# The second feed-forward layer's seven-product chunks: the 256 last token columns of each half, from plain products to seven products of their own

## The chip, the cores and the metric

The kernel runs on one core of a Trainium2 chip. The metric is device microseconds of one execution; a kernel's time is the median of its runs. A core has five engines that run side by side, each through its own queue in order: PE (TensorE, matrix products), DVE (VectorE), ACT (ScalarE), POOL (GpSimd) and SP (SyncE, which issues the transfers). They wait for each other by semaphores.

## The reference

Three stages follow one another: clustered attention over 2 x 8 heads, a mixture of four experts, and a second feed-forward layer. The change is in the last stage, for 1536 tokens, 512 channels and 2048 hidden units:

```python
def _moe2_ref(x, w_in, w_out):
    h = x @ w_in                      # (1536, 512) @ (512, 2048)
    g = np.maximum(0.01 * h, h)
    return (g @ w_out).astype(np.float32)
```

`w_in` and `w_out` come as 64-bit floats; the kernel narrows them to 32 bits itself.

## The kernel before, in words

Every 32-bit operand of a product is split into a high part that TensorE's fp32r format holds and the rest, and a product is three matmuls (high x high, high x low, low x high).

Both feed-forward layers run in chunks of 256 hidden units (`FCH`): 16 chunks for the experts (c = 0 to 15, `N1` = 16), 8 for the second layer (c = 16 to 23). A chunk has a first part, h = x @ w1 with its activation, and a second, h @ w2, which is added to `acc`. The first part comes in two forms. The chunks in `PLAIN` (0, 1, 16, 17, 18) multiply directly: 3 token groups x 2 halves of the hidden units x 12 matmuls of 512 columns. The others call `emit_seven`. It cuts the problem into 2 x 2 blocks (two halves of the channels, two halves of the tokens) and does a Strassen-like scheme with seven block products instead of eight. A block product (`product`) is 6 matmuls. A half has 768 tokens (`HT`); a PSUM bank takes 512 columns, so each product is done for block A, the first 512 columns of each half, and the remaining 256 columns of each half are block B, the narrow block.

For the experts' chunks B goes through seven products too (`some_b` is (A, B)). For the second layer's five seven-product chunks, c = 19 to 23, `some_b` is (A,) and `plain_b(f)` does B directly: for each half f of the hidden units, 12 matmuls of 512 columns, the two halves' 256 columns side by side. `plain_b(0)` stands after the first product of A, `plain_b(1)` ahead of its last.

The sums of token blocks that the seven products need (t1 to t4) don't change over a layer's chunks. `input_sums` makes them once per layer: 14 instructions on DVE and 4 on ACT, 18 steps, which the lists `quota` deal out over the plain chunks. In the second layer: 0 and 4 in the first and second part of chunk 16, 4 and 4 in chunk 17, 3 and 3 in chunk 18.

Behind a result of the first part stands this chain. `h_act`: in the second layer ACT writes 0.01 h to g (L669) and DVE takes the larger (L670), or DVE does both at once where the value lies in SBUF already (L667); in the experts' chunks it is one DVE instruction (L665). Then `split`: ACT writes the high part `hhi` (L126) and POOL the low part `hlo` (L127). The second part (`emit_y2` for the second layer) takes 12 groups of 128 tokens in order, i = 0 to 11, with 6 matmuls each: hhi by w2hi, hhi by w2lo, hlo by w2hi, for both halves of the hidden units. Group i = 4 holds tokens 512 to 639, the first of block B. Each ends in a DVE add to `acc` (L1005 in chunk 16, a copy, L1007 later). Eight PSUM banks are shared; `y_bank` and `BANKS` fix which result takes which, so the ninth group (i = 8) takes the bank that i = 3 had.

The order on each engine is the order in which the code is written. Between the products `some(1)` deals out the steps that prepare the next chunk's weights: `weights_narrow` is one ACT instruction (L179) and four on DVE (L180, L183, L186, L189), each over 128 x 1024 elements. `u2`, `u3` and the like are the scheme's partial sums, in tile `part`; `plus` (L906) adds a bank to them.

Of the kernel before, what the change touches and what calls it, by code (L numbers as in the profile page):

```python
# [66 lines left out]
def attention_moe_kernel(  # L67
# [13 lines left out]
    nc = tc.nc  # L81
    B, H, S, D = q.shape
# [12 lines left out]
    KC = DM // 128  # L95
# [22 lines left out]
    def small(n=None):  # L118
        if n is None:
            n = turns[1]  # L120
            turns[1] += 1
        pool, tag = smalls[n % len(smalls)]
        return pool.tile([128, 512], F32, tag=tag, name=tag)

    def split(hi, lo, src, lo_engine):
        nc.scalar.activation(out=hi, in_=src, func=AF.Copy)  # L126
        lo_engine.tensor_tensor(out=lo, in0=src, in1=hi.bitcast(F32), op=ALU.subtract)  # L127


    xhi = keep.tile([128, KC, NT], F32R, name="xhi")  # L130
    xlo = keep.tile([128, KC, NT], F32R, name="xlo")
# [23 lines left out]
    hbuf, gbuf, pbuf = [], [], []  # L155
# [3 lines left out]
    N1 = len(chunks)  # L159
# [407 lines left out]
    ps = small()  # L567
# [88 lines left out]
    def g_slot(n):  # L656
        return gbuf[n // 2][:, n % 2, :]
# [5 lines left out]
    def h_act(c, g, src, p):  # L663
        if c < N1:
            nc.vector.scalar_tensor_tensor(out=g, in0=src, scalar=0.0, in1=p, op0=ALU.max, op1=ALU.mult)  # L665
        elif src is g:
            nc.vector.scalar_tensor_tensor(out=g, in0=src, scalar=0.01, in1=src, op0=ALU.mult, op1=ALU.max)  # L667
        else:
            nc.scalar.activation(out=g, in_=src, func=AF.Copy, scale=0.01)  # L669
            nc.vector.tensor_tensor(out=g, in0=src, in1=g, op=ALU.max)  # L670

    def h_whole(c, f, src, t0, g=None):

        ts = slice(t0, t0 + 512)
        g = g_next() if g is None else g
        h_act(c, g, src, pbuf[0][:, 0, ts])
        hi, lo = [x[:, f, ts] for x in hbuf[0]]
        split(hi, lo, g, nc.gpsimd)
# [130 lines left out]
    part = ffn.tile([128, 2, NT // 2], F32, name="part")  # L809
# [3 lines left out]
    def bank(n):  # L813
        return psum_f.tile([128, 512], F32, tag=f"z{n}", name=f"z{n}")
# [8 lines left out]
    HT = NT // 2  # L823
# [4 lines left out]
    def input_sums(whole):  # L828

        sub, add = ALU.subtract, ALU.add  # L830
        steps = []

        def tt(out, in0, in1, op):
            steps.append(lambda: nc.vector.tensor_tensor(out=out, in0=in0, in1=in1, op=op))

        cols = slice(0, 512 if whole else HT)

        def parts(n, src):
            hi, lo = t_hi[n][:, :, cols], t_lo[n][:, :, cols]
            steps.append(lambda: nc.scalar.activation(out=hi, in_=src, func=AF.Copy))  # L840
            tt(lo, src, hi.bitcast(F32), sub)

        b11, b12, b21, b22 = [[x.bitcast(F32)[:, :, cols] for x in b] for b in quarters]
        if whole:
            f, g = pbuf[0][:, 0, 0:1024].rearrange("p (k t) -> p k t", k=2), part[:, :, 0:512]
        else:
            f, g = [
                x.bitcast(F32).rearrange("p a b -> p (a b)")[:, 0:NT].rearrange("p (k t) -> p k t", k=2) for x in raw64
            ]
        tt(f, b12[0], b11[0], sub)  # L850
        tt(f, f, b12[1], add)
        tt(f, f, b11[1], sub)
        tt(g, b22[0], f, sub)
        tt(g, g, b22[1], add)
        parts(0, f)
        tt(f, b21[0], g, sub)
        tt(f, f, b21[1], add)
        parts(1, g)
        parts(3, f)
        tt(g, b22[0], b12[0], sub)  # L860
        tt(g, g, b22[1], add)
        tt(g, g, b12[1], sub)
        parts(2, g)
        return steps

    def product(ps, w, x, sub, first=True):

        for k in range(2):
            for i, j in ((0, 0), (0, 1), (1, 0)):
                nc.tensor.matmul(  # L870
                    ps, lhsT=w[i][:, k, :], rhs=x[j][:, k, sub], start=first and k + i + j == 0,
                    stop=k == 1 and i == 1, skip_group_check=True,
                )
# [10 lines left out]
    def emit_seven(c, steps):  # L884

        w = w1s[0]
        a11, a12, a21, a22 = [
            [x[:, 2 * k:2 * k + 2, 128 * f:128 * f + 128] for x in w] for f in range(2) for k in range(2)
        ]
        s1, s2, s3, s4 = [[x[:, n] for x in (shi, slo)] for n in range(4)]  # L890
        t1, t2, t3, t4 = zip(t_hi, t_lo)
        x11, x21, x22 = quarters[0], quarters[2], quarters[3]
        A, B = slice(0, 512), slice(512, HT)
        z = {(A, n): bank(b) for n, b in zip("aebcd", (2, 3, 4, 5, 6))}
        z.update({(B, n): bank(b)[:, 0:256] for n, b in zip("aeb", (0, 1, 7))})
        z[B, "c"], z[B, "d"] = z[B, "b"], z[B, "a"]
        u2, u3 = [{A: part[:, n, A], B: part[:, n, B]} for n in range(2)]
        gB = [g_slot(2), g_slot(3)]

        def some(n):  # L900
            for _ in range(n):
                if steps:
                    steps.pop(0)()

        def plus(out, ps, other):
            nc.vector.tensor_tensor(out=out, in0=ps, in1=other, op=ALU.add)  # L906

        def done(m, f, u, src):
            if m == A:
                h_whole(c, f, src, HT * u, g_slot(0))  # L910
                return
            to = src if f and u else gB[f][:, 256 * u:256 * u + 256]
            h_act(c, to, src, pbuf[0][:, 0, HT * u + 512:HT * u + HT])
            if u == 1:
                hi, lo = [x[:, f, :].rearrange("p (u t) -> p u t", u=2)[:, :, 512:HT] for x in hbuf[0]]
                split(hi, lo, gB[f].rearrange("p (u t) -> p u t", u=2), nc.gpsimd)

        some_b = (A, B) if c < N1 else (A,)

        def plain_b(f):  # L920

            ps = bank(f)
            xs = [x.rearrange("p k (u t) -> p k u t", u=2) for x in (xhi, xlo)]
            for k in range(KC):
                for i, j in ((0, 0), (0, 1), (1, 0)):
                    nc.tensor.matmul(  # L926
                        ps.rearrange("p (u t) -> p u t", u=2), lhsT=w[i][:, k, 128 * f:128 * f + 128],
                        rhs=xs[j][:, k, :, 512:HT], start=k + i + j == 0, stop=k == KC - 1 and i == 1,
                    )
            h_act(c, gB[f], ps, None)  # L930
            hi, lo = [x[:, f, :].rearrange("p (u t) -> p u t", u=2)[:, :, 512:HT] for x in hbuf[0]]
            split(hi, lo, gB[f].rearrange("p (u t) -> p u t", u=2), nc.gpsimd)

        for m in some_b:
            product(z[m, "a"], a11, x11, m)
            nc.scalar.activation(out=u2[m], in_=z[m, "a"], func=AF.Copy)
        weights_split(1)
        some(1)
        if c >= N1:
            plain_b(0)  # L940
            some(1)
        for m in some_b:
            product(z[m, "b"], s2, t2, m)
            plus(u2[m], z[m, "b"], u2[m])
        some(1)
        for m in some_b:
            product(z[m, "a"], a12, x21, m, False)
            done(m, 0, 0, z[m, "a"])
        some(1)
        for m in some_b:  # L950
            product(z[m, "c"], s3, t3, m)
            plus(u3[m], z[m, "c"], u2[m])
        g = g_slot(1)
        c22 = {A: g, B: gB[1][:, 256:512]}
        for m in some_b:
            product(z[m, "e"], a22, t4, m)
            plus(z[m, "e"], z[m, "e"], u3[m])
            if m == A and c < N1:
                done(m, 1, 0, z[m, "e"])
            product(z[m, "d"], s1, t1, m)  # L960
            plus(c22[m], z[m, "d"], u3[m])
        done(B if c < N1 else A, 1, 0, z[B if c < N1 else A, "e"])
        h_act(c, g, g, pbuf[0][:, 0, HT:HT + 512])
        split(hbuf[0][0][:, 1, HT:HT + 512], hbuf[0][1][:, 1, HT:HT + 512], g, nc.gpsimd)
        if c < N1:
            done(B, 1, 1, c22[B])
        else:
            plain_b(1)
        for m in some_b:
            product(z[m, "d"], s4, x22, m, False)  # L970
            plus(z[m, "d"], z[m, "d"], u2[m])
            done(m, 0, 1, z[m, "d"])
# [46 lines left out]
    for c in range(NCH):  # L1019
# [8 lines left out]
        if c in PLAIN:  # L1028
# [6 lines left out]
            if c == N1:  # L1035
                sums_left = input_sums(True)
                quota = [0, 4, 4, 4, 3, 3]
# [7 lines left out]
            for n, (u, f) in enumerate(blocks):  # L1045
                if c > 0:
                    ps = bank(BANKS[u][f])
# [6 lines left out]
                if c == 0:  # L1054
                    ps = both_ps[f]
# [64 lines left out]
```

## Time and profile before

| | |
|---|---|
| median of 3 runs | 1029.95 us (1029.0 to 1031.38) |
| profiled execution, time | 1032.72 us |
| profiled execution, span of the trace | 1031.0 us |
| busy: PE, DVE, POOL, ACT | 1003.8, 715.0, 605.2, 403.8 us |
| mean granted TensorE clock | 0.993 |

A matmul's shown duration overlaps the next one's; what a matmul takes of the engine is the distance between two starts. The time of a row is from the span's start. In a row of several instructions (x2, x3) the busy time is their sum.

### The profile page before, as it was taken

The numbers are of one execution on the slowest core, as the hardware profiler recorded it, in microseconds if no ns is written. First come the engines' busy times: TensorE is split into PE (matmuls) and PEld (weight loads), VectorE is DVE, ScalarE is ACT, GpSimd is POOL, SyncE is SP. The second block draws the span as 40 slices with busy tenths as digits, with TensorE's granted clock in tenths as the row PEclk, the third lists the DMA queues.
The fourth block names the chain that finished last, engine by engine and source line by source line (L and its number), as shares of the span: only waits on it lengthen the run. The fifth ranks groups of instructions, "written<-read, shape, count | busy, mean of one in ns | idle before, by whom it ended". The sixth has DMA issues, their size and how long they took to land.

```text
span 1031.0 us, 15762 instructions
## 1 busy us (share of the span) xinstructions
PE 1003.8 (97%) x6322; PEld 831.3 (81%) x6322; DVE 715.0 (69%) x1066; ACT 403.8 (39%) x562; POOL 605.2 (59%) x460
## 2 busy tenths in 40 slices
PE   7799999999999999999999999999999999999998
PEld 5578888888778888888888888888877888888886
DVE  7698888887778556554565555565678878686664
ACT  3477777775232222221222212222343533334331
POOL 4267777780467657545666546575585646676661
PEclk9799999999999999999999999999999999999999
DMA  7755666540101121011110112012012221212103
GB/s 171 179 109 129 139 140 140 116 124 22 41 21 42 37 56 42 21 41 41 51 42 21 42 41 70 23 55 89 1 41 82 82 82 42 81 41 75 49 1 123
DMA packets 59538, 70.78 MB, mean 69 GB/s; under 512 B 25060, under 2 KB 42088, under 8 KB 59464
## 3 DMA queue, kind: packets, MB, share of 16 engines
q1 hardware_dynamic: 59464, 69.77, 25.4%
q8 instruction: 49, 0.80, 0.3%
q14 instruction: 25, 0.20, 0.1%
HBM read 46.19 MB, written 3.17 MB: 48 GB/s over the span
## 4 chain that ended last, share of the span: by engine, by line
PE 86%; DVE 9%; SPq 2%; issue 1%; POOL 1%; ACT 1%; DMA 0%; DVEq 0%; ACTq 0%; POOLq 0%
PE z L870 24%; PE z L982 8%; PE z L984 8%; PE z L983 8%; PE z L880 6%; PE z L1000 4%; PE z L1002 4%; PE z L1001 4%; PE big L422 3%; PE z L926 3%; PE big L457 3%; PE big L458 2%; DVE m L426 2%; PE small L483 1%; PE small L484 1%; PE small L485 1%
## 5 line engine op out<-in xcount | busy, mean ns | idle before, releaser
L127 POOL TENSOR_TENSOR hlo<-g,hhi 128x512 fp32r<-128x512 f32 x140 | 196.3, 1417 | 143.3 <-ACT hhi L126 138.7
L989 DVE TENSOR_TENSOR acc<-z,acc 128x512 f32<-128x512 f32 x180 | 123.1, 689 | 98.2 <-PE z L984 98.2
L471 POOL TENSOR_TENSOR plo<-p,phi 128x768 f16<-128x768 f32 x84 | 137.9, 1653 | 80.0 <-ACT phi L470 51.9
L126 ACT ACTIVATE hhi<-g 128x512 fp32r<-128x512 f32 x140 | 86.9, 632 | 197.5 <-DVE g L665 154.5
L982 PE MATMUL z<-hhi,w2hi 128*128 128x512 f32 x384 | 153.0, 398 | 1.1 <-DVE acc L987 1.1
L984 PE MATMUL z<-hlo,w2hi 128*128 128x512 f32 x384 | 151.5, 394 | 1.1 <-POOL hlo L127 1.1
L983 PE MATMUL z<-hhi,w2lo 128*128 128x512 f32 x384 | 150.7, 392 | 0.0
L199 POOL TENSOR_TENSOR w2lo<-w2raw,w2hi 128x512 fp32r<-128x512 f32 x46 | 59.0, 1305 | 132.8 <-ACT w2hi L196 132.8
L426 DVE TENSOR_REDUCE m<-big 128x1 f32<-128x768 f32 x96 | 90.0, 951 | 23.7 <-PE big L422 23.4
L460 ACT ACTIVATE p<-big 128x768 f32<-128x768 f32 x96 | 77.4, 808 | 35.0 <-PE big L458 29.6
L984 PEld LDWEIGHTS z<-hlo,w2hi 128*128 128x128 f32 x384 | 72.1, 188 | 19.9 <-POOL hlo L127 1.5
L982 PEld LDWEIGHTS z<-hhi,w2hi 128*128 128x128 f32 x384 | 72.1, 188 | 17.5 <-DVE acc L987 1.5
L983 PEld LDWEIGHTS z<-hhi,w2lo 128*128 128x128 f32 x384 | 72.1, 188 | 16.5
L1000 PE MATMUL z<-w2hi,hhi 128*128 128x512 f32 x192 | 76.5, 398 | 1.2 <-DVE acc L1005 1.0
L1002 PE MATMUL z<-w2hi,hlo 128*128 128x512 f32 x192 | 76.1, 396 | 0.0
L1001 PE MATMUL z<-w2lo,hhi 128*128 128x512 f32 x192 | 76.0, 396 | 0.0
L199 POOL TENSOR_TENSOR w1lo<-w1raw,w1hi 128x512 fp32r<-128x512 f32 x48 | 74.0, 1564 | 1.7 <-ACT w1hi L196 1.6
L457 PE MATMUL big<-qka 128*128 128x512 f32 x192 | 71.7, 374 | 1.6 <-DVE pair L127 0.8
L906 DVE TENSOR_TENSOR part<-z,part 128x512 f32<-128x512 f32 x66 | 38.1, 578 | 50.6 <-PE z L870 50.0
L196 ACT ACTIVATE shi<-sums 128x1024 fp32r<-128x1024 f32 x19 | 20.1, 1060 | 125.6 <-POOL sums L217 125.6
L1007 DVE TENSOR_TENSOR acc<-z,acc 128x512 f32<-128x512 f32 x84 | 56.6, 684 | 17.4 <-PE z L1002 16.6
L665 DVE SCALAR_TENSOR_TENSOR g<-z,pb 128x512 f32<-128x512 f32 x92 | 52.2, 568 | 22.7 <-PE z L870 12.9
(210 smaller groups left out, 2585.1 us busy)
## 6 DMA issues: line engine op xcount, KB each, us to landing
qkb<-pair SPq DMA_DIRECT2D x32, 384.0 KB
w1raw<-in_moe_w_dram SPq DMA_DIRECT2D x16, 512.0 KB
w2raw<-in_moe_w_dram SPq DMA_DIRECT2D x16, 512.0 KB
w1raw<-in_moe_w_in_dram SPq DMA_DIRECT2D x8, 1024.0 KB
w2raw<-in_moe_w_out_dram SPq DMA_DIRECT2D x8, 1024.0 KB
qka<-pair SPq DMA_DIRECT2D x16, 384.0 KB
vraw<-in_v_dram SPq DMA_DIRECT2D x16, 192.0 KB
pb<-pe_rows SPq DMA_DIRECT2D x4, 768.0 KB
```

The lines of the kernel that those rows point to most:

```text
L127: lo_engine.tensor_tensor(out=lo, in0=src, in1=hi.bitcast(F32), op=ALU.subtract)
L199: nc.gpsimd.tensor_tensor(out=lo[:, x], in0=src[:, x], in1=hi.bitcast(F32)[:, x], op=ALU.subtract)
L426: nc.vector.tensor_reduce(out=m_t[t][:, j:j + 1], in_=ps[:, 0:S], op=ALU.max, axis=AX.X)
L471: (nc.vector if plo_on_vector else nc.gpsimd).tensor_tensor(out=plo, in0=p, in1=phi, op=ALU.subtract)
L870: nc.tensor.matmul(ps, lhsT=w[i][:, k, :], rhs=x[j][:, k, sub], start=first and k + i + j == 0, stop=k == 1 and i == 1, skip_group_check=True,
L982: nc.tensor.matmul(ps, lhsT=whi[:, f, ks], rhs=hi[:, f, us], start=f == 0, stop=False)
L983: nc.tensor.matmul(ps, lhsT=wlo[:, f, ks], rhs=hi[:, f, us], start=False, stop=False)
L984: nc.tensor.matmul(ps, lhsT=whi[:, f, ks], rhs=lo[:, f, us], start=False, stop=f == NF - 1)
L989: nc.vector.tensor_tensor(out=a, in0=ps, in1=a, op=ALU.add)
L1000: nc.tensor.matmul(ps, lhsT=hi[:, f, ts], rhs=whi[:, f, :], start=f == 0, stop=False)
L1001: nc.tensor.matmul(ps, lhsT=hi[:, f, ts], rhs=wlo[:, f, :], start=False, stop=False)
L1002: nc.tensor.matmul(ps, lhsT=lo[:, f, ts], rhs=whi[:, f, :], start=False, stop=f == NF - 1)
```

## The change

In the five chunks c = 19 to 23, block B goes through the seven products as in the experts' chunks; `plain_b` is gone. `input_sums` makes the second layer's sums for all 768 columns of a half instead of the first 512.

```diff
@@ input_sums @@
-        cols = slice(0, 512 if whole else HT)
+        cols = slice(0, HT)
...
-            f, g = pbuf[0][:, 0, 0:1024].rearrange("p (k t) -> p k t", k=2), part[:, :, 0:512]
+            f, g = pbuf[0][:, 0, :].rearrange("p (k t) -> p k t", k=2), part[:, :, :]
@@ emit_seven @@
-        some_b = (A, B) if c < N1 else (A,)
-
-        def plain_b(f):
-
-            ps = bank(f)
-            xs = [x.rearrange("p k (u t) -> p k u t", u=2) for x in (xhi, xlo)]
-            for k in range(KC):
-                for i, j in ((0, 0), (0, 1), (1, 0)):
-                    nc.tensor.matmul(
-                        ps.rearrange("p (u t) -> p u t", u=2), lhsT=w[i][:, k, 128 * f:128 * f + 128],
-                        rhs=xs[j][:, k, :, 512:HT], start=k + i + j == 0, stop=k == KC - 1 and i == 1,
-                    )
-            h_act(c, gB[f], ps, None)
-            hi, lo = [x[:, f, :].rearrange("p (u t) -> p u t", u=2)[:, :, 512:HT] for x in hbuf[0]]
-            split(hi, lo, gB[f].rearrange("p (u t) -> p u t", u=2), nc.gpsimd)
-
-        for m in some_b:
+        for m in (A, B):
             product(z[m, "a"], a11, x11, m)
...
         if c >= N1:
-            plain_b(0)
             some(1)
-        for m in some_b:
+        for m in (A, B):
             product(z[m, "b"], s2, t2, m)
             plus(u2[m], z[m, "b"], u2[m])
...
-        done(B if c < N1 else A, 1, 0, z[B if c < N1 else A, "e"])
+        if c >= N1:
+            done(A, 1, 0, z[A, "e"])
+        done(B, 1, 0, z[B, "e"])
         h_act(c, g, g, pbuf[0][:, 0, HT:HT + 512])
         split(hbuf[0][0][:, 1, HT:HT + 512], hbuf[0][1][:, 1, HT:HT + 512], g, nc.gpsimd)
-        if c < N1:
-            done(B, 1, 1, c22[B])
-        else:
-            plain_b(1)
-        for m in some_b:
+        done(B, 1, 1, c22[B])
+        for m in (A, B):
             product(z[m, "d"], s4, x22, m, False)
             plus(z[m, "d"], z[m, "d"], u2[m])
             done(m, 0, 1, z[m, "d"])
```

DVE's queue in one of these chunks, from the first narrowing step of the next chunk's w1 to the partial sum that the last product of A waits for (the second L906 into `g_3471`). Before:

```order
L180 TENSOR_SCALAR w1raw<-w1raw 128x1024
L906 TENSOR_TENSOR part<-z_8847,part 128x512
L183 TENSOR_SCALAR w1raw<-w1raw 128x1024
L670 TENSOR_TENSOR g_3471<-z_8845,g_3471 128x512
L186 SCALAR_TENSOR_TENSOR w1raw<-w1raw_4249,w1raw 128x1024
L906 TENSOR_TENSOR part<-z_8848,part 128x512
L906 TENSOR_TENSOR z_8846<-z_8846,part 128x512
L906 TENSOR_TENSOR g_3471<-z_8849,part 128x512
```

The same stretch of DVE's queue now; the rows of 128x256 are the narrow block's:

```order
L180 TENSOR_SCALAR w1raw<-w1raw 128x1024
L906 TENSOR_TENSOR part<-z_8872,part 128x512
L906 TENSOR_TENSOR part<-z_8877,part 128x256
L183 TENSOR_SCALAR w1raw<-w1raw 128x1024
L670 TENSOR_TENSOR g_3471<-z_8870,g_3471 128x512
L670 TENSOR_TENSOR g_4247<-z_8875,g_4247 128x256
L186 SCALAR_TENSOR_TENSOR w1raw<-w1raw_4249,w1raw 128x1024
L906 TENSOR_TENSOR part<-z_8873,part 128x512
L906 TENSOR_TENSOR part<-z_8877,part 128x256
L906 TENSOR_TENSOR z_8871<-z_8871,part 128x512
L906 TENSOR_TENSOR g_3471<-z_8874,part 128x512
```

Three instructions of the narrow block came in ahead of that partial sum, one of them an L670 that waits for ACT.

ACT's queue at the end of such a chunk, from the high part of A's partial sum on (L126 rows with 128x2x256 are block B's; `g_4247` is B's buffer). Before:

```order
L126 ACTIVATE hhi_3469<-g_3471 128x512 x2
L669 ACTIVATE g_4247<-z_8929 128x512
L126 ACTIVATE hhi_3469<-g_4247 128x2x256
L669 ACTIVATE g_3471<-z_8849 128x512
L126 ACTIVATE hhi_3469<-g_3471 128x512
L179 ACTIVATE w2raw<-w2raw_4250 128x1024
```

And now:

```order
L126 ACTIVATE hhi_3469<-g_3471 128x512
L669 ACTIVATE g_4247<-z_8876 128x256
L126 ACTIVATE hhi_3469<-g_3471 128x512
L126 ACTIVATE hhi_3469<-g_4247 128x2x256
L669 ACTIVATE g_3471<-z_8874 128x512
L126 ACTIVATE hhi_3469<-g_3471 128x512
L669 ACTIVATE g_4247<-z_8875 128x256
L126 ACTIVATE hhi_3469<-g_4247 128x2x256
L179 ACTIVATE w2raw<-w2raw_4250 128x1024
```

The last high part that the chunk makes was A's (second token half); now it is B's, for the first half of the hidden units and both token halves.

## Rows read from the trace of the kernel before

**Rows 1.** The page: busy time of PE, and the chain that ended last.
```profile
PE 1003.8 (97%) x6322; PEld 831.3 (81%) x6322; DVE 715.0 (69%) x1066; ACT 403.8 (39%) x562; POOL 605.2 (59%) x460
PE 86%; DVE 9%; SPq 2%; issue 1%; POOL 1%; ACT 1%; DMA 0%; DVEq 0%; ACTq 0%; POOLq 0%
```
**Rows 2.** Windows: stretch, length, busy us (instructions) of PE PEld DVE ACT POOL, clock, DMA.
```profile
320.19:334.89 14.70, 14.70 (x85) 12.87 (x84) 10.44 (x17) 3.65 (x6) 8.52 (x6) 1.00 0.20 62
779.37:798.42 19.05, 17.88 (x74) 13.23 (x72) 19.00 (x22) 4.32 (x6) 10.13 (x6) 1.00 0.18 56
815.20:832.00 16.80, 16.80 (x74) 13.50 (x73) 15.88 (x20) 5.39 (x7) 6.62 (x4) 1.00 0.04 17
898.07:913.40 15.33, 15.33 (x68) 12.44 (x67) 9.46 (x13) 7.36 (x11) 7.02 (x6) 1.00 0.08 30
```
**Rows 3.** Timeline of PE, an experts' chunk: start, us, instruction, [idle before <-releaser].
```profile
320.19 0.39 PE L870 MATMUL z<-xhi,w1hi 128*128 128x512 f32 x1
321.59 0.28 PE L870 MATMUL z<-xhi,w1hi 128*128 128x256 f32 x1
322.29 0.40 PE L870 MATMUL z<-thi,shi 128*128 128x512 f32 x1
```
**Rows 4.** Timeline of DVE, second part of chunk 16.
```profile
787.07 1.21 DVE L834 TENSOR_TENSOR pb<-xhi 128x1024 f32<-128x1024 f32 x1
...
790.44 0.68 DVE L1005 COPY acc<-z 128x512 f32<-128x512 f32 x1
791.04 1.69 DVE L834 TENSOR_TENSOR pb<-pb,xlo 128x1024 f32<-128x1024 f32 x1
```
**Rows 5.** Timeline of PE, the same stretch.
```profile
791.26 0.47 PE L1000 MATMUL z<-w2hi,hhi 128*128 128x512 f32 x1 [0.48 <-DVE acc L1005]
```
**Rows 6.** L834 by itself: ns min/median/max, first and last start, form (the experts' sums).
```profile
L834 DVE TENSOR_TENSOR w1raw<-w1raw,xlo x3: 1742/1742/1770, 275.8 to 295.8; 128x1536 f32<-128x1536 f32 x3
```
**Rows 7.** Timeline of ACT, the seven-product part of chunk 20.
```profile
899.67 0.60 ACT L936 ACTIVATE part<-z 128x512 f32<-128x512 f32 x1 [4.89 <-PE z L870]
...
901.11 1.12 ACT L179 ACTIVATE w1raw<-w1raw 128x1024 f32<-128x1024 f32 x1
902.48 0.60 ACT L669 ACTIVATE g<-z 128x512 f32<-128x512 f32 x1 [0.25 <-PE z L926]
903.91 0.63 ACT L126 ACTIVATE hhi<-g 128x512 fp32r<-128x512 f32 x1 [0.83 <-DVE g L670]
```
**Rows 8.** Timeline of DVE, the same stretch.
```profile
903.18 0.69 DVE L670 TENSOR_TENSOR g<-z,g 128x512 f32<-128x512 f32 x1 [4.22 <-ACT g L669]
...
906.98 1.21 DVE L186 SCALAR_TENSOR_TENSOR w1raw<-w1raw,w1raw 128x1024 int32<-128x1024 int32 x1
...
908.89 0.70 DVE L906 TENSOR_TENSOR z<-z,part 128x512 f32<-128x512 f32 x1
909.50 0.68 DVE L906 TENSOR_TENSOR g<-z,part 128x512 f32<-128x512 f32 x1
```
**Rows 9.** Timeline of POOL, the same stretch.
```profile
901.29 2.54 POOL L199 TENSOR_TENSOR w2lo<-w2raw,w2hi 128x512 fp32r<-128x512 f32 x2 [3.89 <-ACT w2hi L196]
904.62 1.29 POOL L127 TENSOR_TENSOR hlo<-g,hhi 128x512 fp32r<-128x512 f32 x1 [0.78 <-ACT hhi L126]
```
**Rows 10.** Groups by line and form, 690 to 1031 us, narrow forms: xcount | busy, mean ns.
```profile
L906 DVE TENSOR_TENSOR part<-z,part 128x256 f32<-128x256 f32 x4 | 1.7, 425 | 0.1
...
L936 ACT ACTIVATE part<-z 128x256 f32<-128x256 f32 x2 | 0.8, 384 | 0.2
```
**Rows 11.** Timeline of POOL in chunks 17 and 21.
```profile
804.74 1.28 POOL L127 TENSOR_TENSOR hlo<-g,hhi 128x512 fp32r<-128x512 f32 x1
...
948.59 2.14 POOL L127 TENSOR_TENSOR hlo<-g,hhi 128x512 fp32r<-128x512 f32 x1 [0.85 <-ACT hhi L126]
```
**Rows 12.** Timeline of DVE in chunks 17 and 21.
```profile
805.01 1.56 DVE L180 TENSOR_SCALAR w1raw<-w1raw 128x1024 f32<-128x1024 f32 x1 [1.72 <-ACT w1raw L179]
...
948.35 1.22 DVE L189 SCALAR_TENSOR_TENSOR w1raw<-w1raw,w1raw 128x1024 int32<-128x1024 int32 x1
```

More of the change, by code (lines that the diff above doesn't have):

```diff
@@ L949, in emit_seven @@
         some(1)
-        for m in some_b:
+        for m in (A, B):
             product(z[m, "c"], s3, t3, m)
@@ L954, in emit_seven @@
         c22 = {A: g, B: gB[1][:, 256:512]}
-        for m in some_b:
+        for m in (A, B):
             product(z[m, "e"], a22, t4, m)
@@ L961, in emit_seven @@
             plus(c22[m], z[m, "d"], u3[m])
-        done(B if c < N1 else A, 1, 0, z[B if c < N1 else A, "e"])
+        if c >= N1:
+            done(A, 1, 0, z[A, "e"])
+        done(B, 1, 0, z[B, "e"])
         h_act(c, g, g, pbuf[0][:, 0, HT:HT + 512])
         split(hbuf[0][0][:, 1, HT:HT + 512], hbuf[0][1][:, 1, HT:HT + 512], g, nc.gpsimd)
-        if c < N1:
-            done(B, 1, 1, c22[B])
-        else:
-            plain_b(1)
-        for m in some_b:
+        done(B, 1, 1, c22[B])
+        for m in (A, B):
             product(z[m, "d"], s4, x22, m, False)
```

## The prediction, made before the changed kernel ran

> **What bounds the kernel now.** I read the page first: PE is busy 97% of the span and 86% of the chain that ended last is PE's [rows 1]. So the kernel is PE from end to end, and a change is worth what it takes from PE's queue less the gaps it opens there. The windows come next, for where PE has gaps and how full DVE is in the stretches the change touches [rows 2]. In the seven-product part of chunk 20 (898.07 to 913.40) PE has no gap: 15.33 of 15.33 us, with DVE at 9.46. An experts' chunk, where the narrow block already takes the seven products, is 14.70 us, without a gap either. One stretch is different: the second part of chunk 16 lasts 19.05 us with DVE busy for 19.00 of it. There DVE is the bound, and PE waits for banks: the ninth group starts at 791.26 after DVE's copy of the fourth, which ended at 790.44 + 0.68 [rows 4, 5]. Last I read the timelines of ACT, DVE and POOL in chunk 20, because the change lengthens their chains [rows 7 to 9].
>
> **PE's own work.** A product on 512 columns takes 321.59 - 320.19 = 1.40 us, one on 256 columns 322.29 - 321.59 = 0.70 us [rows 3]: half the columns, half the time. Removed per chunk: 24 matmuls of 512 columns at 1.40 / 6, 5.60 us. Added: 42 of 256 columns at 0.70 / 6, 4.95 us (seven products). That is -0.65 us a chunk, -3.2 us in five, if PE never waits; it agrees with 15.33 against 14.70.
>
> **The sums of token blocks.** 14 DVE instructions grow from 1024 to 1536 elements. At 1024 one takes 1.21 us, or 1.69 beside POOL [rows 4]; the experts' sums at 1536 take 1.742 [rows 6]. So +0.53 each. Four stand in the second part of chunk 16, in the queue between the copies that free PE's banks; DVE has nothing to hide them under, and PE gets 4 x 0.53 = 2.1 us of further gaps. Longer instructions also meet POOL more often there, at most one more difference of 1.69 - 1.21; I take 2.3, bounds 1.6 (three of the four stand ahead of the copy of i = 4) to 2.6. The other ten stand in chunks 17 and 18. In the second part of chunk 17 DVE is busy 15.88 of 16.80 us without a PE gap [rows 2]; PE's groups run five banks ahead of the copies, some 5 x 1.4 us, and two more times 0.53 fit under that. I cost them at nothing; without that cover it would be 10 x 0.53 = 5.3 us, and up to 0.5 of it I keep for the range.
>
> **The chains in a chunk.** The steps between engines, from chunk 20: ACT starts 0.20 us after a product's end (899.67 against 898.07 + 1.40); DVE 0.10 after ACT (902.48 + 0.60 to 903.18); ACT 0.04 after DVE (903.87 to 903.91); POOL 0.08 after ACT (904.54 to 904.62) [rows 7 to 9]; PE 0.14 after DVE [rows 4, 5]. On DVE an instruction starts 0.09 before the last one's end [rows 8]. The narrow L906 takes 0.43, the narrow copy on ACT 0.38 [rows 10]; I use these for narrow L670 and L669 too. POOL's instructions take 1.27 each [rows 9].
>
> DVE and POOL hold each other up where both work in SBUF. L180 at 805.01 met a POOL instruction that ran from 804.74 to 806.02, and ended 0.55 us after it. At 948.35 L189 came first: POOL's instruction of 948.59 took 2.14 and ended 1.16 us after L189's end [rows 11, 12]. So whoever starts first finishes, the other then takes nearly its whole time.
>
> Now the new order, in us from the block's first matmul. (1) ACT's narrow copy waits for its product until 2.31 and pushes L179 from 3.04 to 3.55, done at 4.67; POOL's two w2lo follow from 3.72. (2) DVE's L180 meets the first w2lo and ends at 5.54, the two L906 end at 6.5, L183 meets the second w2lo (to 6.70) and ends at 7.25, L670 of A ends at 7.85. (3) ACT's queue holds L126 of A before L669 of B, so B's L669 runs 8.44 to 8.82 and DVE, whose next instruction is L670 of B, sits idle for 1 us and ends it at 9.35. (4) Meanwhile POOL has begun A's hlo (8.61 to 9.88); L186, which in the trace came ahead of POOL (906.98), now comes behind it and ends at 11.0. (5) Four more L906 follow, and the sum that the last product of A accumulates onto ends at 13.17. PE is there at 12.56 and starts at 13.31: **a gap of 0.75 us**. Before, that sum ended at 909.50 + 0.68, 12.1 [rows 8], and the 2.8 us of `plain_b(1)` stood in between. Queued behind it are B's last product and the whole second part.
>
> (6) The second part starts at 13.31 + 1.37 + 0.71 = 15.39, and its group i = 4, the first of the narrow block, at 15.39 + 4 x 1.40 = 21.0. What it needs is now the last thing the chunk makes. On ACT and DVE it stands behind three rounds of L669, L670, L126: A's of the second half of hidden units (DVE 13.8, ACT done 15.17), B's (DVE done 15.98), the two L667 (the first meets A's hlo on POOL, 15.25 to 16.52, and ends at 17.15; the second at 17.5), L906, L669, L670, L126 of A (ACT done 20.32), then L906, L669 and L670 of B (21.13), and B's L126 from 21.17 to 21.80. POOL could start the low part at 21.88, but DVE has the add of group 0 and then L189, from 21.7 to 22.87; the low part ends at 24.03, as in the row at 948.59. PE waits at i = 4 until 21.85 for the high part (0.85), does two matmuls (0.47), and waits from 22.32 to 24.14 for the low part (1.82): **2.67 us**. Before, the last one was A's second token half, not needed before i = 6.
>
> So chunks 19 to 22 cost -0.65 + 0.75 + 2.67 = +2.8 us each. Chunk 23 prepares no weights: no L180, L183, L186, L189. By the same steps the sum for A's last product is there in time, the high part lands at 21.1 and the low at 22.5, against 20.3 for i = 4: 0.8 + 1.0 = 1.8 of gaps, +1.2 in all. The bounds of a chunk's gaps are 0.0 (an experts' chunk, same products, no gap [rows 2]) and 0.75 + 2.67 + 0.5, the last for one more meeting with POOL.
>
> What no row shows is L667 beside a running POOL instruction. It reads SBUF alone, as L186 and L189 do, so I let it wait as they do; if it does not, everything behind it is 0.55 us earlier, 2.8 us less over five chunks, 1041.8 in all.
>
> The Trainium skill's page "SBUF — State Buffer", section "Who interferes with whom", says that a DVE instruction with both inputs in SBUF contends with a GpSimd instruction that reads SBUF, and that the one issued first keeps the port for its whole length. [...] By it L667 would wait; a reading that lets only the integer instructions wait would give the 1041.8.
>
> **The sum.** -3.2 + 2.3 + 4 x (0.75 + 2.67) + 1.8 = +14.6 us. The profiled execution took 1032.72 us (span 1031.0) and would take 1047.3; it lies 2.77 above the median of the runs shown, 1029.95, so the median goes to 1044.6.
>
> **Rivals.** (a) The narrow chain lands in time. Place: the last product of A and group i = 4; it holds if A's sum ends before 12.4 and B's low part before about 21.4. For it: the experts' chunks do the same products with the same order on PE without a gap. Against: there h_act is one DVE instruction and nothing is narrowed in between, so neither (3) nor (4) exists. Price: -3.2 us, and with the sums' 2.3 it is -0.9, 1029.0; if chunk 16 also absorbs its four instructions, 1026.7. (b) DVE and POOL meet less than I let them. Without any meeting, step (5) ends at 12.40, no gap there, and at i = 4 the high part lands at 20.7 and the low at 22.1 against 20.2: 1.3 us of gaps. -0.65 + 1.3 is +0.7 a chunk, 3.4 in five, with 2.1 for the sums +5.5: 1035.5. For it: the order of two starts 0.1 to 0.7 us apart decides each meeting. Against: L189 and the last low part met in just this way in the trace. (c) The gaps grow: each late part of a chunk delays the next one's weights. POOL's chain in the second part would have to lose over 2 us more; at most 1 us a chunk by the bounds above, 1049.
>
> **Chances.** The forecast with its L667 variant, 1040 to 1047: 65%. (b) and what lies between it and the forecast, 1033 to 1040: 17%. (a) at 1029.0: 6%, at 1026.7: 7%. (c), 1047 to 1051: 5%. A measurement of this kernel tells about 0.2%, 2.1 us, from no change. Faster is (a) without the sums' cost, 7%; the same is (a) with it, 6%; slower is all else, 87%. The range leaves out (a) and the end of (c): 1034 to 1048.5.
>
> **What would show it.** In the second part of chunk 16 PE's stretch of 19.05 us grows to 21.2 to 21.6. In the five chunks the row of `xhi,shi` matmuls of the last product of A shows idle time released by DVE's L906 into g, about 0.75 us in four of the five; in the second part, the first high-part matmul of group i = 4 waits for ACT's L126 and its first low-part matmul for POOL's L127, 0.9 and 1.8 us. A narrow product still takes 0.70 us. If PE shows no idle before i = 4, the forecast is wrong and (a) holds; if the waits are there at half the size, the meetings of DVE and POOL were mis-sized.

## The result, and the profile after

The changed kernel took 1044.89 us (median of 4 runs, 1041.9 to 1047.08), the kernel before, on the same chip, 1029.63 (1029.0 to 1031.38): ratio 1.0147, 95% interval 1.0131 to 1.0162. That is 15.3 us slower; the forecast was 14.6 (1044.6 from 1029.95). (The ratios here and below are estimates from all runs of both kernels; they need not be the quotient of the two medians.) Below, "the layer" is the distance from the first matmul of chunk 16 to the start of the last one: 1026.47 - 762.50 = 263.97 us before, 1040.86 - 760.25 = 280.61 after, +16.6. The part ahead of the layer was 2.2 us shorter in this execution; that belongs to no step of the change, and in the other traces, where that part is the same code, the layer starts anywhere from 757.85 to 761.50.

The page of the kernel after, PE's busy time and the chain, against [rows 1]:

```profile
PE 1005.1 (96%) x6410; PEld 833.0 (80%) x6412; DVE 734.2 (70%) x1101; ACT 404.9 (39%) x572; POOL 617.2 (59%) x460
PE 75%; DVE 14%; POOL 4%; ACT 3%; issue 2%; DMA 1%; SPq 1%; POOLq 0%; DVEq 0%; ACTq 0%
```

PE's share of the chain fell from 86 to 75%; DVE, POOL and ACT took it over. PE's waits in the layer are four groups (engine, line, tile, releaser and its line: us in total, times, longest); no wait for DVE's g or for a part of `hhi` or `hlo` stood in these chunks before:

```profile
PE z L984 <- POOL hlo L127: 6.9, 5, 1.6
PE z L982 <- DVE acc L987: 3.1, 3, 1.5
PE z L870 <- DVE g L906: 2.1, 4, 0.9
PE z L982 <- ACT hhi L126: 1.4, 5, 0.3
```

**Chunk 16.** Windows of the kernel after, for the second parts of chunks 16 and 17 and the two parts of chunk 20 (columns as in [rows 2]):

```profile
777.12:798.28 21.16, 17.88 (x73) 13.23 (x72) 21.12 (x22) 4.32 (x6) 11.17 (x6) 1.00 0.16 51
815.13:831.90 16.77, 16.77 (x73) 13.49 (x72) 16.77 (x19) 6.49 (x7) 10.30 (x4) 1.00 0.04 14
902.41:917.81 15.40, 15.00 (x85) 12.94 (x84) 9.36 (x16) 5.97 (x10) 4.57 (x4) 1.00 0.06 22
917.81:937.06 19.25, 17.40 (x74) 13.34 (x73) 16.45 (x23) 6.34 (x9) 16.61 (x13) 1.00 0.28 82
```

The first grew from 19.05 to 21.16, with DVE full in both; the second, where DVE now fills all of the 16.77 us, gave PE no gap. DVE's sums in chunk 16 and the wait of the ninth group, against [rows 4, 5]:

```profile
787.07 2.25 DVE L834 TENSOR_TENSOR pb<-pb,xlo 128x1536 f32<-128x1536 f32 x1
789.23 0.68 DVE L987 COPY acc<-z 128x512 f32<-128x512 f32 x1
```
```profile
790.06 0.47 PE L982 MATMUL z<-w2hi,hhi 128*128 128x512 f32 x1 [1.53 <-DVE acc L987]
```

Beside POOL a sum now takes 2.25 instead of 1.69, and the wait is 1.53 instead of 0.48.

**The chunks 19 to 23.** PE in chunk 20: the last product of A, and the first high and first low part of group i = 4.

```profile
915.58 0.50 PE L870 MATMUL z<-xhi,shi 128*128 128x512 f32 x1 [0.40 <-DVE g L906]
...
923.88 0.50 PE L982 MATMUL z<-w2hi,hhi 128*128 128x512 f32 x1 [0.28 <-ACT hhi L126]
...
926.18 0.50 PE L984 MATMUL z<-w2hi,hlo 128*128 128x512 f32 x1 [1.57 <-POOL hlo L127]
```

The idle time shown is less than a wait costs. The distance between starts, beyond the usual 0.234 (0.117 behind a matmul of 256 columns, as ahead of the first of the three), is 0.67, 0.55 and 1.83 here, each with 0.1 at the start that follows. These are the two waits forecast. What feeds them, on DVE, ACT and POOL, against [rows 7 to 9]:

```profile
909.60 0.68 DVE L670 TENSOR_TENSOR g<-z,g 128x512 f32<-128x512 f32 x1
911.25 0.43 DVE L670 TENSOR_TENSOR g<-z,g 128x256 f32<-128x256 f32 x1 [0.97 <-ACT g L669]
911.60 1.81 DVE L186 SCALAR_TENSOR_TENSOR w1raw<-w1raw,w1raw 128x1024 int32<-128x1024 int32 x1
...
914.86 0.68 DVE L906 TENSOR_TENSOR g<-z,part 128x512 f32<-128x512 f32 x1
...
918.10 1.61 DVE L667 SCALAR_TENSOR_TENSOR g<-g 128x512 f32<-128x512 f32 x2
...
923.68 1.32 DVE L189 SCALAR_TENSOR_TENSOR w1raw<-w1raw,w1raw 128x1024 int32<-128x1024 int32 x1
```
```profile
910.32 0.63 ACT L126 ACTIVATE hhi<-g 128x512 fp32r<-128x512 f32 x1 [1.49 <-DVE g L670]
910.85 0.37 ACT L669 ACTIVATE g<-z 128x256 f32<-128x256 f32 x1
...
923.20 0.63 ACT L126 ACTIVATE hhi<-g 128x512 fp32r<-128x512 f32 x1 [0.49 <-DVE g L670]
```
```profile
911.03 1.29 POOL L127 TENSOR_TENSOR hlo<-g,hhi 128x512 fp32r<-128x512 f32 x1 [1.90 <-ACT hhi L126]
...
917.53 1.30 POOL L127 TENSOR_TENSOR hlo<-g,hhi 128x512 fp32r<-128x512 f32 x1 [5.21 <-ACT hhi L126]
...
920.12 6.01 POOL L127 TENSOR_TENSOR hlo<-g,hhi 128x512 fp32r<-128x512 f32 x4 [1.29 <-ACT hhi L126]
```

ACT's order puts L126 of A (910.32) ahead of L669 of B (910.85), so DVE idles 0.97; POOL's `hlo` then starts 0.57 ahead of L186, which takes 1.81; and the sum for A's last product ends at 914.86 + 0.68 = 915.54, while PE's last matmul before it started at 914.90.

**What was not forecast: the clock.** In chunks 19 and 22, not in 20 and 21, PE ran behind the wait at i = 4 at half pace: starts 0.43 apart instead of 0.234. Windows of the kernel after behind that wait in chunk 19 and in chunk 20 (the last three columns are the granted clock, the DMA share and GB/s):

```profile
890.30:894.30 4.00, 4.00 (x12) 3.14 (x11) 3.96 (x6) 0.00 (x0) 3.92 (x4) 0.57 0.68 244
924.30:928.30 4.00, 2.43 (x11) 1.75 (x10) 4.00 (x6) 1.64 (x2) 3.90 (x3) 1.00 0.53 146
```

The first is mostly at the lower of the clock's two levels, 1.2 GHz, the second at 2.4. Eight matmuls of 0.2 us more each: 1.6 us a stretch.

### The profile page after: what moved, and what is told of

It reads as the page before. It is cut to its first block, busy times and chain, and to the rows that moved or that the text cites. A ratio compares the mean times of both kernels' runs of the same rounds, so it can differ in the third digit from the quotient of the medians.

```text
span 1045.4 us, 15998 instructions
## 1 busy us (share of the span) xinstructions
PE 1005.1 (96%) x6410; PEld 833.0 (80%) x6412; DVE 734.2 (70%) x1101; ACT 404.9 (39%) x572; POOL 617.2 (59%) x460
## 4 chain that ended last, share of the span: by engine, by line
PE 75%; DVE 14%; POOL 4%; ACT 3%; issue 2%; DMA 1%; SPq 1%; POOLq 0%; DVEq 0%; ACTq 0%
PE z L870 21%; PE z L964 8%; PE z L966 8%; PE z L965 8%; PE z L880 6%; POOL hlo L127 4%; PE big L422 3%; PE z L984 3%; PE big L457 3%; PE z L982 2%; PE z L983 2%; PE big L458 2%; DVE m L426 2%; PE small L483 1%; PE small L484 1%
## 5 line engine op out<-in xcount | busy, mean ns | idle before, releaser
L127 POOL TENSOR_TENSOR hlo<-g,hhi 128x512 fp32r<-128x512 f32 x140 | 199.1, 1438 | 153.3 <-ACT hhi L126 149.6
L126 ACT ACTIVATE hhi<-g 128x512 fp32r<-128x512 f32 x140 | 86.5, 631 | 205.2 <-DVE g L665 154.6
L906 DVE TENSOR_TENSOR part<-z,part 128x512 f32<-128x512 f32 x76 | 41.5, 555 | 53.3 <-PE z L870 52.7
L199 POOL TENSOR_TENSOR w1lo<-w1raw,w1hi 128x512 fp32r<-128x512 f32 x48 | 76.9, 1623 | 2.0 <-ACT w1hi L196 1.6
```

The lines of the kernel that those rows point to most:

```text
L199: nc.gpsimd.tensor_tensor(out=lo[:, x], in0=src[:, x], in1=hi.bitcast(F32)[:, x], op=ALU.subtract)
```

## The experiments

The theory was: the layer grows by three things, sums that crowd DVE in chunk 16, L186 stuck behind B's narrow copy and POOL, and block B's last activations standing at the end of three engines' queues when i = 4 wants them. The main rivals: the sums' cost lies elsewhere, the meetings of DVE and POOL are not what prices the waits, the waits pass work from one place to another whatever is repaired. All times are medians beside runs of the kernel before on the same chip.

**1. The sums alone.** The kernel before, with the sums over 768 columns (the last one stored for 512), `plain_b` kept.

```diff
-        cols = slice(0, 512 if whole else HT)
+        cols = slice(0, HT)
...
```

> The kernel before, with only the token sums made for all 768 columns (the last one is stored for the first 512 columns only, since plain_b still reads what lies behind them); the chunks keep plain_b. Theory: the sums cost what chunk 16's second part shows, 19.05 to 21.2 us, and nothing in chunks 17 and 18: +2.1 us, about 1031.8. Rival (DVE's throughput is the cost of the whole change): 13 of 14 instructions are 0.53 us longer, and some of the backlog shows in chunks 17 to 19 too: +4 to +7 us, 1034 to 1037.

1032.05 us against 1029.77: ratio 1.0023 (1.0013 to 1.0033), +2.3. PE's waits in chunk 16 are those of the changed kernel, 1.54, 1.01 and 0.60, and there is no other in the layer. The window of chunk 16's second part has the changed kernel's 21.16 us:

```profile
776.28:797.44 21.16, 17.87 (x73) 13.23 (x72) 21.12 (x22) 4.31 (x6) 11.17 (x6) 1.00 0.16 51
```

The term of the sums is shown by itself.

**2. Each token half of B split as soon as it is there**, in the changed kernel, instead of both at the end.

```diff
-            if u == 1:
+            if c >= N1:
+                ts = slice(HT * u + 512, HT * u + HT)
+                split(hbuf[0][0][:, f, ts], hbuf[0][1][:, f, ts], to, nc.gpsimd)
+            elif u == 1:
```

> The changed kernel, but in chunks 19 to 23 the narrow block's two token halves are split into high and low part one by one, each as soon as it is there, instead of together after the second: two narrow L126 and two narrow POOL instructions in place of one of each. Theory: group i = 4 needs the first token half only, which is ready before the last products, so the gap ahead of i = 4 (2.4 us in four chunks, 1.3 in the last) goes, and with it the stretches at the half clock that followed it (1.6 us each in two chunks): about 1044.9 - 11 = 1034, or 1031 to 1034 with the clock. The second half is needed at i = 10, 14 us later. The 0.7 us gap ahead of the last product of A stays. Rival (the chains on ACT, DVE and POOL are simply too long, whatever stands last): POOL gets more instructions, the wait moves to i = 0 to 3 or to i = 10, and less than 4 us come back: above 1040.

1033.61 us, ratio 1.0029 (1.0012 to 1.0045). Every wait at i = 4 is gone, with it the half clock; the one ahead of A's last product stays in chunks 19 to 22, here that of chunk 20:

```profile
912.17 0.50 PE L870 MATMUL z<-xhi,shi 128*128 128x512 f32 x1 [0.40 <-DVE g L906]
```

So 11 of the 15 us hung on one `if`: the narrow split waited for the second half, and that was the last thing the chunk made.

**3. L189 two additions later in chunks 19 to 22**, by four empty steps ahead of it, in the changed kernel; the second part's steps behind L189 move with it.

```diff
+        if N1 + 2 < c < NCH - 1:
+            steps = 4 * [lambda: None] + steps
```

> The changed kernel, but in chunks 19 to 22 the next chunk's L189 stands two adds later in DVE's queue, behind the add of group 2 instead of group 0. Theory (L189 takes the SBUF side from POOL just when the narrow block's last low part is due): POOL starts it at once, and PE's wait for it falls from 1.74 to about 0.8 us in these four chunks: -3.6 us, more if the half-clock stretches go too, 1038 to 1041.5. Rival (the chain up to the high part sets it, L189's place does nothing): same as the changed kernel, 1044 to 1046.

1039.51 us, ratio 1.0103 (1.0087 to 1.0118). The wait for the low part, in chunk 20:

```profile
924.05 0.51 PE L984 MATMUL z<-w2hi,hlo 128*128 128x512 f32 x1 [0.64 <-POOL hlo L127]
```

1.57 became 0.64 in all four chunks, what the last chunk, which has no L189, shows in the changed kernel too (0.63). L189 kept POOL from its last piece by some 0.93 us, the meeting of [rows 11, 12] again, and no half clock followed the shorter waits.

**4. L186 out of the first part**, in the changed kernel; it then stands in the second part.

```diff
-        some(1)
+        if c < N1:
+            some(1)
```

> The changed kernel, but in chunks 19 to 22 L186 (the next chunk's third narrowing step) no longer stands between the L670 and the partial sums; it is dealt out in the second part, ahead of L189. Theory: the partial sum that the last product of A accumulates onto is ready 1.7 us earlier, and the gap ahead of it (1.13, 0.67, 0.67, 0.66 us) goes; the last low part then meets L186 in place of L189, and the gap at i = 4 stays about as it is: -2 to -4 us, 1041 to 1043. Rival (the sum waits for ACT's L669 of the narrow block, and L186 is hidden in it): the gap stays at 0.5 us or more, 1044 to 1046.

1041.61 us, ratio 1.0119 (1.0095 to 1.0143). The gap ahead of A's last product is gone in every chunk (the second part starts 14.70 us after the first), that at i = 4 is unchanged (1.57 idle for the low part). The windows of chunk 20's two parts:

```profile
898.89:913.59 14.70, 14.70 (x86) 12.89 (x84) 7.91 (x14) 6.43 (x11) 6.97 (x6) 1.00 0.07 29
913.59:932.99 19.40, 17.55 (x75) 13.33 (x73) 17.02 (x24) 5.88 (x10) 15.15 (x11) 1.00 0.29 87
```

So L186 was the price of the first gap.

**5. Repairs 2 and 4 together.**

> The changed kernel with two edits together: each token half of the narrow block is split as soon as it is there, and L186 is dealt out in the second part. Theory: the chunks' three terms add up, so with both waits gone only PE's -3.2 us (less any rest of the waits) and the sums' +2.1 to +2.3 us in chunk 16 are left: 1028.5 to 1029.5, the same as the kernel before. Rival (there is a floor below which the longer chains open another gap, at i = 0 or 1 behind A's high part): 1031 or more.

A miss: 1036.98 us against 1029.94, ratio 1.0069 (1.0053 to 1.0085), slower than repair 2 alone. The rival's 1031 or more holds by its number, but not at the place that it named. Both old waits are gone. New ones stand in the second parts of chunks 19 to 21 and in the first parts of 20 to 23, here those of chunks 19 and 20:

```profile
890.70 0.51 PE L986 MATMUL z<-w2hi,hhi 128*128 128x512 f32 x1 [0.37 <-DVE acc L993]
...
900.04 0.50 PE L870 MATMUL z<-thi,slo 128*128 128x512 f32 x1 [0.44 <-POOL slo L199]
```

In the second part L186 delays DVE's additions, which free PE's banks, and with L189 behind it the next chunk's weights: POOL's sums of them start at 893.50, and `slo`, the low part of these sums, comes too late for the second product. I had counted what L186 frees and not what it pushes. In run 4 POOL's sums start as late behind the beginning of the second part (14.79 us there, 14.73 here), but with the wait at i = 4 that part is 19.38 us long and not 18.10, so they were still in time.

**6. As 5, and all four wide sums out of chunk 16** (`quota` from [0, 4, 4, 4, 3, 3] to [0, 0, 4, 5, 5, 4]: one step more in chunk 17 and three in 18).

> As the run with both edits, and the 18 steps of the token sums dealt out as 0, 0, 4, 5, 5, 4 over the parts of chunks 16 to 18 in place of 0, 4, 4, 4, 3, 3, so none stands in the second part of chunk 16. Theory: that part's gaps (2.2 us before, 4.3 with the wide sums) go, and the chunks' -3.2 us shows whole: about 1029.8 - 3.2 - 2.2 = 1024.4, if DVE's fuller parts of chunks 17 and 18 open less than 1 us of gaps. Rival (DVE is the bound over chunks 16 to 18 as a whole, so the steps cost the same wherever they stand): 1028.5 to 1029.5, as without that edit.

A miss too: 1041.31 us, ratio 1.0111 (1.0092 to 1.013), far above what theory and rival gave. The waits of 5 are still there, chunk 16 keeps one of 0.42, and chunks 17 and 18 now wait, the longest:

```profile
828.54 0.50 PE L986 MATMUL z<-w2hi,hhi 128*128 128x512 f32 x1 [1.21 <-DVE acc L993]
...
862.12 0.77 PE L986 MATMUL z<-w2hi,hhi 128*128 128x512 f32 x1 [2.60 <-DVE acc L993]
```

The second is followed by a stretch of half clock.

**7. The same list in the kernel before**, with its sums of 512 columns.

> The kernel before, with the 18 steps of its token sums (512 columns of each half) dealt out as 0, 0, 4, 5, 5, 4 in place of 0, 4, 4, 4, 3, 3. Theory: the second part of chunk 16 falls from 19.05 to about 16.9 us and nothing opens elsewhere: -2.2 us, 1027.6. Rival: the gaps there come from the backlog that DVE brings along from narrowing w1, not from the sums, and at least 1 us of them stays: 1028.6 or more.

1029.31 us, ratio 0.9989 (0.9976 to 1.0002): not told from no change, and not the 1027.6 expected; the rival's 1028.6 or more fits. In the trace the second part of chunk 16 went from 19.05 to 17.55 us, so 0.7 of its gaps stayed; the second parts of chunks 18 and 19 grew by 0.15 and 0.27, too little for the list of waits, and the layer is 262.87 us, 1.1 less than before. Chunks 17 and 18 hold more sums of 1024 elements nearly for nothing; those of 1536 they do not.

**8. The changed kernel, profiled once more.**

> The changed kernel, unedited, profiled once more. Theory: the waits at i = 4 come back alike in every chunk (2.2 to 2.3 us in four, 1.3 in the last), while the stretches of half clock behind them do not belong to a chunk: other chunks than 19 and 22, or another number of them, and the time moves by 1.6 us for each. Rival: the half clock belongs to what runs in chunks 19 and 22, and they show it again.

1045.47 us in one run. The waits are the same, group by group, to 0.1 us. The half clock stood in neither 19 nor 22 but behind the wait of chunk 20; windows of this run, chunk 20 and the same place in chunk 19:

```profile
926.10:928.20 2.10, 2.10 (x6) 1.66 (x5) 1.45 (x3) 0.00 (x0) 2.10 (x3) 0.50 0.95 371
890.80:893.40 2.60, 2.60 (x13) 2.08 (x12) 2.60 (x5) 0.00 (x0) 2.60 (x2) 1.00 0.96 362
```

Six matmuls in 2.10 us and thirteen in 2.60, in stretches as full of transfers (0.95 and 0.96): neither the chunk nor a high DMA load by itself decides it.

**9. Repair 2, and L186 moved into DVE's idle time**, between A's L670 and B's.

```diff
-        some(1)
+            if m == A and c >= N1:
+                some(1)
+        if c < N1:
+            some(1)
```

> After, with each token half of B's activations split as soon as it is there (as in the run that split each half early) and with L186 of w1 moved between the L670 of A and of B of the first block, into the 1 us in which DVE waits for ACT's copy of B. Theory of the crowded second part: L186 stays out of the second part, ends 1.7 to 1.9 us earlier than in after, and the gap ahead of A's last product goes (1.13 + 3 x 0.67 = 3.1 us) with no new gap in the y part: 1033.6 - 3.1 = 1030.5, within 1029 to 1031.5, no gaps in chunks 19 to 23. Rival, the two repairs exclude each other wherever L186 stands: gaps at the first y additions and at the next block's slo as in the run with both repairs, 1035 to 1037.

1029.82 us against 1029.77, ratio 0.9999 (0.999 to 1.0008). The list of waits has none in chunks 19 to 23. DVE in chunk 20 of this kernel, and the windows of its two parts:

```profile
903.84 0.68 DVE L670 TENSOR_TENSOR g<-z,g 128x512 f32<-128x512 f32 x1
904.44 1.21 DVE L186 SCALAR_TENSOR_TENSOR w1raw<-w1raw,w1raw 128x1024 int32<-128x1024 int32 x1
905.57 0.41 DVE L670 TENSOR_TENSOR g<-z,g 128x256 f32<-128x256 f32 x1
...
908.04 0.69 DVE L906 TENSOR_TENSOR g<-z,part 128x512 f32<-128x512 f32 x1 [0.53 <-PE z L870]
```
```profile
896.64:911.36 14.72, 14.72 (x85) 12.82 (x84) 9.27 (x16) 7.33 (x12) 7.92 (x7) 1.00 0.18 69
911.36:928.37 17.01, 17.01 (x74) 13.49 (x73) 15.56 (x23) 5.61 (x11) 15.18 (x12) 1.00 0.23 65
```

L186 now takes 1.21, not 1.81, in time in which DVE had only waited, and the sum (908.04) waits for PE, not PE for it. A chunk is 31.73 us against 32.16 before: 0.43 of the 0.65 that the forecast takes off for PE. The first part gives 0.58 (14.72 against 15.30); 0.15 is lost again in the second (17.01 against 16.86), where the last low-part matmul of i = 0 and the one behind it start 0.29 and 0.34 us after their predecessors instead of 0.234. Five chunks like this about pay for the wide sums in chunk 16, and the layer is 263.96 us, as before.

**10. The changed kernel with that move of L186 alone**, without repair 2.

> After with only L186 of w1 moved between the L670 of A and of B. Theory: the gap ahead of A's last product goes in chunks 19 to 22 (about 3 us), the i = 4 gap of 2.2 to 2.4 us stays in each, so 1041 to 1042 (half clock stretches add or leave up to 1.6 us each). Rival: the sum waits for ACT's copy of B, not for L186, and the gap stays at 0.5 to 0.7 us each, 1044 to 1045.

1040.33 us, ratio 1.0103 (1.0083 to 1.0123), a little under the 1041 to 1042 expected: the first gap goes, that at i = 4 stays (1.57 idle), one stretch of half clock.

**11. As 9, and two of the wide sums out of chunk 16** (`quota` [0, 2, 4, 5, 4, 3]: since the steps keep their order, chunks 17 and 18 hold one step more each).

> The kernel with the early split and the moved L186, and two of the four steps of the wide sums moved from the second part of chunk 16 to that of chunk 17 (quota [0, 2, 4, 5, 4, 3]). Theory that chunk 17 has room for one more pair (DVE busy 15.9 of 16.8 us before): chunk 16's gaps fall by about 2 us, none elsewhere, 1028 to 1028.8, below the kernel before. Rival, DVE is the bound over the whole of chunks 16 to 18 with sums on 768 columns: what chunk 16 gives back shows as gaps in the second parts of 17 or 18, 1030 to 1033.

The rival held: 1033.15 us, ratio 1.003 (1.0019 to 1.0041). Chunk 16's second part falls from 21.15 to 19.08 us, but chunks 17 and 18 wait:

```profile
827.16 0.50 PE L988 MATMUL z<-w2hi,hhi 128*128 128x512 f32 x1 [0.42 <-DVE acc L995]
...
863.19 0.47 PE L988 MATMUL z<-w2hi,hhi 128*128 128x512 f32 x1 [2.79 <-DVE acc L995]
```

The work has to leave DVE, not only the chunk.

**12. As 9, and chunk 16's twelve copies into `acc` on ACT.**

```diff
-            nc.vector.tensor_copy(out=a, in_=ps)
+            nc.scalar.activation(out=a, in_=ps, func=AF.Copy)
```

> The kernel with the early split and L186 moved into DVE's wait, and in chunk 16 the twelve copies of the second part's banks into acc on ACT instead of DVE. Theory that only DVE's queue opens the gaps of chunk 16: DVE loses 12 x 0.6 = 7.2 us of its 21.1 us there, ACT (busy 4.3 of 21.15 us) takes about 12 x 0.57; the second part falls from 21.15 to 16.9 us, no gap elsewhere, 1029.8 - 4.3 = 1025.5, below both kernels. Rival, ACT's queue takes DVE's place: the copy of the second group stands behind ACT's high part of w1 (L196, 782.88, which waits for DVE's L189), and the banks come free late: gaps of 1 to 2 us stay, 1026.5 to 1027.5. Rival, sums on 768 columns load DVE too much over chunks 16 to 18 wherever they stand, as the run with the moved quota showed: gaps in chunks 17 and 18, 1028 or more.

1026.57 us against 1030.06, ratio 0.9967 (0.9955 to 0.9979): 0.3% faster than the kernel before, and so faster than both. The list of the layer's waits is empty, and it takes 1020.39 - 760.72 = 259.67 us, 4.29 less than in 9, as expected. The medians show 3.5 against the kernel before; that number alone would fit the first rival too (1026.5 to 1027.5), and it is the trace, without a gap in chunk 16, that rules it out. The second parts of chunks 16 and 17:

```profile
777.59:794.46 16.87, 16.87 (x73) 13.56 (x72) 16.66 (x11) 10.00 (x17) 11.09 (x6) 1.00 0.19 64
811.33:828.19 16.86, 16.86 (x73) 13.56 (x72) 16.65 (x19) 6.79 (x8) 11.28 (x5) 1.00 0.10 38
```

21.15 became 16.87. DVE is still nearly full there (16.66), but what it does in that time no longer frees PE's banks. Some 2.2 us of the gain, the gaps that chunk 16 had before the change, could probably be had in the kernel before by these copies alone; that was not run.

## Why the prediction was right

- **PE's own work**, -0.65 a chunk. Chunk 23's first part, which has no gap, is 14.69 us from first matmul to first matmul, against 15.30 before (the 15.33 of [rows 2] ends a little past that start): -0.61. The mechanism is right and the size nearly. Its own sum was off by as much: 42 times 0.70 / 6 is 4.90, not 4.95, and would have given -0.70.
- **The sums**, 2.3 forecast, bounds 1.6 to 2.6. 21.16 - 19.05 = 2.11 in the profile, 2.28 between the medians of run 1. That chunks 17 and 18 take ten longer instructions for nothing held: 67.47 us before, 67.48 after. It was nearer the edge than the argument knew: two sums more cost 5.9 us in these two chunks, a stretch of half clock among them (run 11).
- **The gap ahead of A's last product**, 0.75. It is about 0.67 in chunks 20 to 22, and step by step as worked out: L186 ends 11.00 us after the block's start (11.0 forecast), the sum at 13.13 (13.17). In chunk 19 it is 1.13: there L189 of w2 ends only 2.99 us into the block, and ACT's `w2hi`, which waits for it, starts at 3.02 instead of 2.59, which I had not looked at. Runs 4, 9 and 10 show the cause, L186: the gap goes wherever L186 is moved to.
- **The wait at i = 4**, 0.85 + 1.82. Measured 0.55 + 1.83. The high part was over-sized by 0.30: B's last L670 ended at 20.75, not 21.13, a lead that grew from 0.13 us at A's high part over the rounds behind it. That L189 is in the low part's price was worked out and is shown by run 3. L667 does wait for POOL: the pair starts at 918.10, POOL's `hlo` ends at 918.83, and the pair takes 1.61, where the one of 512 columns took 0.68 without POOL in the kernel before. That only integer instructions wait was unlikely from the rows: L180 works on f32 and reads one tensor, and it took 1.56 beside POOL [rows 12] against 0.69 without. The two rows without POOL, in the kernel before:

```profile
903.79 0.69 DVE L180 TENSOR_SCALAR w1raw<-w1raw 128x1024 f32<-128x1024 f32 x1
...
910.93 0.68 DVE L667 SCALAR_TENSOR_TENSOR g<-g 128x512 f32<-128x512 f32 x1
```

- **Chunk 23**, +1.2: 32.93 - 31.93 = +1.0.
- **What the sum lacked** is the clock. The parts above make +13.5 in the layer, and two stretches of half clock another 3.1: 16.6. That the forecast of the median came within 0.3 us is in part luck: its terms were over-sized by about 1.1 us together, and a cost of 1.6 to 3.1 us, which it did not have, made up for that.
- **The rivals.** (a), the chain in time, was false as the code stood, and its price was nearly right: run 9, where the chain is in time, gives 1029.82 where (a) with the sums had 1029.0. The order of the queues that the forecast took as given is one that two small edits mend. (b) and (c) are out: the meetings were there, and the gaps do not grow from chunk 20 to 21.

## What to carry to other kernels

Half the columns is a gain only as long as the chain that makes the next part's first operand is no longer than what it replaces; write down who needs it first and where it stands in each engine's queue, and split what is needed first as soon as it is there. When a repair frees an instruction, price its new place as carefully as its old one: the free time to look for is that in which the same engine waits anyway. And where a full engine frees the banks, move that small copy to an idle engine before moving large work in time.

## What the runs showed of the hardware

The half clock was not expected. Behind some of PE's longer waits in this layer, in an engine otherwise busy from end to end, the granted clock fell to about half for eight matmuls, which then started 0.43 us apart instead of 0.234; that cost about 1.6 us each time. In the layer's traces it followed two of the four waits of 1.56 to 1.58 us in the changed kernel, one of four in its second profile and in run 10, none of four in run 4, and the waits of 2.60 and 2.79 in runs 6 and 11. It followed none of the waits of 1.53 or 1.54 us in chunk 16, nor any shorter one. That is no threshold: the two kinds differ by a few hundredths of a microsecond and stand in different surroundings, each i = 4 wait having another of 0.55 us just ahead of it. What decides it among like waits is not settled. In this kernel a wait like those at i = 4 cost up to 1.6 us beyond its own length.
